# Attention with a top-32 mask and a feed-forward network in one kernel: a slot's transposes, the values of the slot ahead and later scores are put behind one another on TensorE

## The chip, the cores and the metric

The kernel runs on one core of one Trainium2 chip. The metric is the time of one execution in microseconds (us) as the device measures it. The core's engines are TensorE (PE in the rows; PEld are its weight loads), VectorE (DVE), ScalarE (ACT), GpSimd (POOL) and the queue that issues transfers (SP). Each works through its own instructions in order and waits on semaphores for the others.

## The reference

```python
# q, k, v: batch 8, heads 8, sequence 576, head_dim 64, float32
scores = scale * np.matmul(q, k.transpose(0, 1, 3, 2))
kth = np.partition(scores, -32, axis=-1)[..., -32:-31]
scores = np.where(scores >= kth, scores, -1e9)
scores = scores - np.max(scores, axis=-1, keepdims=True)
attn = np.exp(scores)
attn = attn / (np.sum(attn, axis=-1, keepdims=True) + 1e-09)
x = np.matmul(attn, v)                 # heads side by side: 4608 tokens x 512
a, b = x @ w1, x @ w2                  # 512 x 1024 each
out = (a * b @ w3) @ w_out             # 1024 x 1024, 1024 x 512
```

## The kernel before, in words

The work is cut into **slots**. A slot is 128 query rows of one pair of heads of one batch entry (or, at the ends of the sequence, 64 rows of two pairs). There are 18 slots per batch entry and 144 in all. Twelve slots fill a **block**: 384 columns of x, for which the feed-forward network is then computed with 288 matmuls of 384 columns. The weights w3 and w_out are folded into one matrix at the start, and weights, x and g are split into a high and a low part, so that three matmuls stand for one product.

One round p of the main loop (line 514) works on four slots at once, each at another stage. The scores of slot p+1 are made by `scores` (TensorE, into two tiles st) and copied to s by `take_scores` (ScalarE), in two halves. The 32 largest values of slot p are found by `top32_steps` (VectorE), whose parts the loop calls with `next(finder)`. For slot j = p-1, `edges_of` (GpSimd) prepares threshold and maximum, `mask` (ScalarE, then GpSimd) masks, and `exps` (ScalarE) takes the exponentials and their sums, head by head. For slot m = p-2, `invert` (VectorE) and `normalise` (ScalarE) divide, `turn` transposes the weights on TensorE (eight transposes into tp, a ninth, the tail, into ro), `take_turned` (ScalarE) copies both out as pts and pr, and `values` (TensorE) multiplies them with v. The result ov is split into x by `split_high` (ScalarE) and `split_low` (VectorE).

Between these stages `fill(8)` stands three times a round. It first calls `evict`, which issues the copies and products that wait for finished feed-forward groups (asb, g, osb: ScalarE, VectorE, GpSimd), and then 8 matmuls of the block whose turn it is. `begin` takes a finished block into that queue. `warm` does the same for the loading and decoding of weights, in the first rounds alone; in those no feed-forward runs. Every instruction keeps the order of the program on its engine (class `InOrder`), so what stands in the loop is what each engine does, in that order.

The tiles tp and st share a pool of two buffers in PSUM (`ps_a`); ro and ov share one. The array of TensorE is used whole (128x128) by the transposes and the feed-forward, as two halves of 64 rows (64x128) by the scores, and as two halves of 64 columns (128x64) by the values.

Of the kernel before, what the change touches and what calls it, by code (L numbers as in the profile page):

```python
# [9 lines left out]
F32 = mybir.dt.float32  # L10
# [8 lines left out]
B, H, S, D = 8, 8, 576, 64  # L19
# [49 lines left out]
def attn_moe(ctx: ExitStack, tc: tile.TileContext, q, k, v, w1, w2, w3, w_out, out, flag, any_missed, general):  # L69
# [39 lines left out]
    def stir(n):  # L109
        idle = ps_e.tile([128, 512], F32, tag="pf", name="idle", bufs=1)  # L110
        for _ in range(n):
            pe.matmul(idle[:, :128], ident, ident, start=True, stop=True)
# [69 lines left out]
    def at(x, b, *i):  # L182
        return x[(b, *i)] if isinstance(b, int) else x[(ds(b, 1), *i)].rearrange("o p n -> (o p) n")

    def load_q(b, t, split=False):
        qt = att_p.tile([128, NHP * 128], F32, tag="q", name="qt")
        for cut in (slice(0, 128), slice(128, NHP * 128)) if split else (slice(0, NHP * 128),):
            sp.dma_start(qt[:, cut], at(q, b, t)[:, cut])
        return qt

    def load_k(b, hp):
# [69 lines left out]
        return edge  # L261

    def new_weights():
        return att_p.tile([128, 2, S], F32, tag="pab", name="pab"), small.tile([128, 2], F32, tag="sums", name="sums")

    def mask(s, edge, pab, a, after=None):
        act.activation(pab[:, a, :], s[:, a, :], AF.Relu, bias=edge[:, a, 1:2], scale=-STEEP)
# [18 lines left out]
        for a in range(2):  # L286
            act.activation(pab[:, a, :], pab[:, a, :], AF.Copy, scale=rec[:, a : a + 1])

    def turn(pab):
        tp = ps_a.tile([128, 2, 512], F32, tag="a", name="tp")  # L290
        flat = pab[:].rearrange("p a c -> p (a c)")
        for a in range(2):
            for c in range(4):
                o = a * (S + 64) + c * 128
                pe.transpose(tp[:, a, c * 128 : (c + 1) * 128], flat[:, o : o + 128], ident)
        ro = ps_v.tile([128, 512], F32, tag="v", name="ro")
        pe.transpose(ro[:, :128], flat[:, 512:640], ident)
        return tp, ro

    def take_turned(tp, ro):  # L300
        pts = att_p.tile([128, 2, 512], F32, tag="pts", name="pts", bufs=1)
        act.copy(pts, tp)
        pr = att_p.tile([128, 128], F32, tag="pr", name="pr", bufs=1)
        act.copy(pr, ro[:, :128])
        return pts, pr

    def values(vts, hps, pts, pr, ro):
        ov = ro[:, 256:384]
        ends = len(hps) == 2
        for j, hp in enumerate(hps):  # L310
            vt = vts[hp]
            for c in range(5):
                for i, h in enumerate(HEADS):
                    block = i * 4 + c if c < 4 else (((8, 10), (10, 9))[j][i] if ends else 8 + i)
                    n = HEADS[i ^ j] if ends else slice(0, 128)
                    rhs = pr[:, n] if c == 4 else pts[:, j if ends else i, c * 128 + n.start : c * 128 + n.stop]
                    to = ov[h, j * 64 : j * 64 + 64] if ends else ov[h]
                    pe.matmul(to, vt[:, block * D : (block + 1) * D], rhs, start=(c == 0), stop=(c == 4))
        return ov
# [14 lines left out]
    def split_low(high, low, whole):  # L334
        dve.tensor_tensor(low, whole, high.bitcast(F32), op=ALU.subtract)
# [49 lines left out]
    if general:  # L385
        outs = out.rearrange("e (b t) -> b e t", b=B)
        for src, step in startup:
            for _ in step(fetch(src)):
                pass
        settle()  # L390
        with tc.For_i(0, B, 1) as b:
            seen = small.tile([1, 1], I32, tag="seen", name="seen", bufs=1)
            nc.sync.dma_start(seen, flag[ds(b + 1, 1), :])
            with tc.If(nc.values_load(seen, min_val=0, max_val=1) > 0):
                kts = {hp: load_k(b, hp) for hp in range(NHP)}
                vts = {hp: load_v(b, hp) for hp in range(NHP)}
                for first, ts in ((0, range(3)), (NB, range(3, TAIL + 1))):
                    xs, lo = [new_x(0) for _ in range(NHP)], 0
                    for t in ts:
                        qt = load_q(b, t)  # L400
                        for hps in [hps for hps, u in slots_of(0) if u == t]:
                            s, st = new_s(), scores(qt, kts, hps)
                            for h in range(2):
                                take_scores(s, st, h)
                            edge = top32_exact(s)
                            pab, sums = new_weights()
                            for a in range(2):
                                mask(s, edge, pab, a)
                                exps(edge, pab, sums, a)
                            add_up(sums)  # L410
                            invert(sums)
                            normalise(pab, sums)
                            tp, ro = turn(pab)
                            pts, pr = take_turned(tp, ro)
                            ov = values(vts, hps, pts, pr, ro)
                            for part in parts_of([xs[hp] for hp in hps], lo, t, ov):
                                split_high(*part)
                                split_low(*part)
                        lo += width(t)
                    place = lambda es: outs[ds(b, 1)][:, es, first : first + lo].rearrange("o p n -> (o p) n")  # L420
                    for _ in moe_steps(xs, lo, [(place, slice(0, lo))], lambda f: f()):
                        pass
        return
# [57 lines left out]

    def renew_q(g):
        if g < len(groups):
            qts[g] = load_q(*groups[g], g == 0)

    waiting = list(startup)
    fetched, going = [], []
# [16 lines left out]
        prefetch(WAITING)  # L504

    renew_q(0)
    stir(8)
    kts[0, 0] = load_k(0, 0)
    prefetch(4)
    kts[0, 1] = load_k(0, 1)  # L510
    kts[0, 2] = load_k(0, 2)
    kts[0, 3] = load_k(0, 3)
    renew_q(1)
    for p in range(-1, n_slots + 3):
        i, j, m = p + 1, p - 1, p - 2
        if p == 1:
            vts[0, 0] = load_v(0, 0)
            vts[0, 1] = load_v(0, 1)
            vts[0, 2] = load_v(0, 2)
            vts[0, 3] = load_v(0, 3)  # L520
        finder = top32_steps(ss[p], p) if 0 <= p < n_slots else iter(())
        if 0 <= m < n_slots:
            invert(pabs[m][1])
        folded = next(finder, None)
        for part in fresh:
            split_low(*part)
        fresh.clear()
        warm()
        if 0 <= j < n_slots:
            edges[j] = edges_of(j)  # L530
        if 0 <= m < n_slots:
            normalise(*pabs[m])
        if 0 <= j < n_slots:
            pabs[j] = new_weights()
            for a in range(2):
                mask(ss[j], edges[j], pabs[j][0], a, folded if a == 0 else None)
        warm()
        fill(SHARE[0])
        begin()
        next(finder, None)  # L540
        if 0 <= m < n_slots:
            tp, ro = turn(pabs[m][0])
            pts, pr = take_turned(tp, ro)
        if 0 <= j < n_slots:
            exps(edges[j], *pabs[j], 0)
        warm()
        fill(SHARE[1])
        next(finder, None)
        warm()
        if i < n_slots:  # L550
            b, hps, t = slots[i]
            st = scores(qts[group_of[i]], of(kts, b), hps)
            ss[i] = new_s()
            take_scores(ss[i], st, 0)
        if 0 <= j < n_slots:
            exps(edges[j], *pabs[j], 1)
        if i < n_slots:
            take_scores(ss[i], st, 1)
            renew(kts, load_k, i)
            if i + 1 == n_slots or group_of[i + 1] != group_of[i]:  # L560
                renew_q(group_of[i] + 2)
        if 0 <= m < n_slots:
            b, hps, t = slots[m]
            ov = values(of(vts, b), hps, pts, pr, ro)
            renew(vts, load_v, m)
        if p == 13:
            stir(9)
        next(finder, None)
        warm()
        fill(SHARE[2])  # L570
        for _ in finder:
            pass
        if 0 <= m < n_slots:
            n = m // BLOCK
            for hp in hps:
                if (n, hp) not in xs:
                    xs[n, hp] = new_x(n)
            fresh += parts_of([xs[n, hp] for hp in hps], column[group_of[m]], t, ov)
            for part in fresh:
                split_high(*part)  # L580
            del ss[m], pabs[m], edges[m]
            if (m + 1) % BLOCK == 0:
                starting.append(n)
        if p == 2:
            stir(8)
        if 0 <= j < n_slots:
            add_up(pabs[j][1])
        warm()
    begin()
# [67 lines left out]
```

## Time and profile before

| | |
|---|---|
| median of 3 runs | 1254.57 us (1254.1 to 1254.63) |
| the profiled execution's own time | 1254.34 us |
| its span, first to last instruction | 1252.4 us |
| TensorE busy | 1211.6 us (97%) |
| VectorE busy | 1147.6 us (92%) |
| ScalarE busy | 1107.9 us (88%) |
| GpSimd busy | 693.0 us (55%) |

The span counts from the first instruction to the last; the time of an execution holds a little more around it. A busy engine is one with an instruction under way; since instructions overlap, busy time says little of the room that is left, and the starts of successive instructions say more. The first 165 us belong to the decoding of weights, the last 50 us to the feed-forward of the last block alone; between them lie 130 slots of equal make.

### The profile page before, as it was taken

The page shows a single profiled execution, that of the slowest core. Times are in us where ns is not written, and L with a number is a line of the kernel's source. Part 1 is how long each engine was busy: PE and PEld are TensorE (multiplying, and loading weights), DVE is VectorE, ACT ScalarE, POOL GpSimd, SP SyncE. Part 2 cuts the span into 40 slices and gives each one's busy share as a digit, 9 for nine tenths or more (in the row PEclk, how much of TensorE's full clock was granted, in tenths as well). Part 3 has the DMA queues.
Part 4 walks back from the last instruction along what each step waited for, and adds up shares of the span by engine and source line. Part 5 has one row for each costly group of instructions (what it writes and reads, how often), then busy time and mean ns, then how long its engine had stood idle before and what let it go on. Part 6 is the DMA issues. An engine that isn't in the chain of part 4 may idle for free.

```text
span 1252.4 us, 27210 instructions
## 1 busy us (share of the span) xinstructions
PE 1211.6 (97%) x9419; PEld 1032.4 (82%) x9419; DVE 1147.6 (92%) x3952; ACT 1107.9 (88%) x2233; POOL 693.0 (55%) x877
## 2 busy tenths in 40 slices
PE   3899799999999999999999999999999999999998
PEld 2554378888888888888888888888888888888998
DVE  7999999999999999999999999999999999999710
ACT  5899999999999999999999999999999999999921
POOL 3688766556556556556556556556556556556510
PEclk7899899999999999999999999999999999999999
DMA  7344302000210012000210012000210012000000
GB/s 289 110 144 152 109 32 84 21 24 21 75 46 10 22 45 84 22 23 21 76 46 10 23 45 83 22 23 21 76 46 10 23 46 84 22 23 1 14 13 27
DMA packets 30258, 64.71 MB, mean 52 GB/s; under 512 B 5412, under 2 KB 11812, under 8 KB 30116
## 3 DMA queue, kind: packets, MB, share of 16 engines
q1 hardware_dynamic: 30116, 62.93, 15.4%
q8 instruction: 75, 1.23, 0.4%
q14 instruction: 67, 0.55, 0.1%
HBM read 53.48 MB, written 9.44 MB: 50 GB/s over the span
## 4 chain that ended last, share of the span: by engine, by line
PE 88%; DVE 5%; ACT 4%; POOL 2%; issue 1%; POOLq 0%; ACTq 0%
PE ab L58 34%; PE eo L58 17%; PE ro L58 15%; PE st L58 12%; PE tp L58 9%; ACT pab L58 2%; DVE w L58 2%; POOL z L58 1%; DVE top L58 1%; ACT z L58 1%; DVE z L58 1%; ACT pts L58 1%; POOL wl L58 1%; DVE t L58 1%; PE pf L58 1%
## 5 line engine op out<-in xcount | busy, mean ns | idle before, releaser
L58 POOL TENSOR_TENSOR pab<-s,pab 128x576 f32<-128x576 f32 x288 | 404.9, 1427 | 247.5 <-ACT pab L58 229.3
L58 DVE MAX8 top<-w 128x8 f32<-128x192 f32 (+1 forms) x1152 | 467.3, 447 | 0.0
L58 PE MATMUL ab<-x,wh 128*128 128x384 f32 x1536 | 402.9, 343 | 0.3 <-DVE wl L58 0.3
L58 DVE MATCH_REPLACE8 w<-top,w 128x192 f32<-128x192 f32 x864 | 289.7, 343 | 0.0
L58 PEld LDWEIGHTS ab<-x,wh 128*128 128x128 f32 x1536 | 273.9, 188 | 0.5 <-DVE wl L58 0.5
L58 PE MATMUL ab<-x,wl 128*128 128x384 f32 x768 | 268.4, 350 | 0.0
L58 ACT ACTIVATE pab<-pab,edge 128x576 f32<-128x576 f32 x288 | 227.1, 789 | 1.8 <-POOL pab L58 1.8
L58 PE MATMUL eo<-g,wf 128*128 128x384 f32 x1152 | 225.6, 345 | 0.0
L58 ACT ACTIVATE pab<-pab,sums 128x576 f32<-128x576 f32 x288 | 211.3, 795 | 8.2 <-DVE sums L58 8.1
L58 ACT COPY pts<-tp 128x1024 f32<-128x1024 f32 x144 | 145.9, 1013 | 74.1 <-PE tp L58 73.9
L58 ACT ACTIVATE pab<-s,edge 128x576 f32<-128x576 f32 x288 | 208.7, 784 | 1.9 <-POOL edge L58 1.9
L58 PEld LDWEIGHTS eo<-g,wf 128*128 128x128 f32 x1152 | 198.5, 188 | 7.5 <-issue 7.5
L58 PE MATMUL st<-kt,qt 64*128 64x288 f32 (+1 forms) x1280 | 186.0, 436 | 10.2 <-ACT pts L58 5.4
L58 ACT COPY s<-st 128x576 f32<-128x576 f32 x288 | 185.0, 643 | 8.7 <-PE st L58 8.7
L58 PEld LDWEIGHTS ro<-pts,vt 128*64 128x64 f32 x2560 | 128.9, 138 | 57.0 <-ACT g L58 34.7
L58 PE MATMUL tp<-ident,pab 128*128 128x128 f32 x1152 | 152.3, 276 | 18.7 <-ACT pab L58 18.7
L58 DVE TENSOR_TENSOR w<-s 128x384 f32<-128x384 f32 x288 | 150.4, 562 | 15.8 <-ACT s L58 7.7
L58 DVE TENSOR_TENSOR w<-w,s 128x384 f32<-128x384 f32 x288 | 159.4, 553 | 4.9
L58 PE MATMUL ro<-pts,vt 128*64 128x128 f32 (+1 forms) x2560 | 163.0, 271 | 0.0
L58 POOL TENSOR_TENSOR g<-asb,g 128x384 fp32r<-128x384 f32 x96 | 96.7, 1008 | 119.6 <-ACT g L58 119.6
L58 PEld LDWEIGHTS tp<-ident,pab 128*128 128x128 f32 x1152 | 135.9, 142 | 31.6 <-ACT pab L58 24.7
L58 PEld LDWEIGHTS ab<-x,wl 128*128 128x128 f32 x768 | 143.9, 187 | 13.4 <-issue 12.3
(50 smaller groups left out, 1133.1 us busy)
## 6 DMA issues: line engine op xcount, KB each, us to landing
z<-in_w SPq DMA_DIRECT2D x32, 512.0 KB, 3.6
vt<-in_v SPq DMA_DIRECT2D x32, 352.0 KB, 3.4
kt<-in_k SPq DMA_DIRECT2D x32, 320.0 KB, 3.2
qt<-in_q SPq DMA_DIRECT2D x39, 256.0 KB, 2.7
out_t<-osb SPq DMA_DIRECT2D x32, 192.0 KB, 1.9
z<-in_wo SPq DMA_DIRECT2D x8, 512.0 KB, 6.6
out_t<-osb SPq DMA_DIRECT2D x16, 160.0 KB, 1.8
out_t<-osb SPq DMA_DIRECT2D x16, 32.0 KB, 1.6
```

The lines of the kernel that those rows point to most:

```text
L58: ins = fn(*args, **kw)
```

## The change

From the slot after the first block to the last but one (`together(m)`), the order within a round is another.

- The tail is transposed ahead of the other eight (`turn(pab, ahead)`), into the tile vo, and pr is copied at once, by `take_tail`. The second head's mask goes behind it on ScalarE.
- `values` of the slot ahead (m-1, so p-3) stand right behind the transposes, and the scores of slot p+1 right behind these. All 24 feed-forward matmuls of a round follow one another.
- ro and ov were a tile that is taken anew in each slot; they are now two places in one lasting tile, vo.
- The exponentials of the second head stand ahead of `split_high` and the evictions of the second `fill`; the second half of the score copies is the last that ScalarE does in a round. `split_low` goes to the end of VectorE's search.
- pts is written over the slot's own weights pab, which therefore have three buffers, pr two. q has one buffer, is loaded in one transfer and a group later than before. At the start 6 instead of 8 matmuls of the identity are issued.

The flags `True` and `False` in the loop are constants.

```diff
-    def load_q(b, t, split=False):
-        qt = att_p.tile([128, NHP * 128], F32, tag="q", name="qt")
-        for cut in (slice(0, 128), slice(128, NHP * 128)) if split else (slice(0, NHP * 128),):
-            sp.dma_start(qt[:, cut], at(q, b, t)[:, cut])
+    def load_q(b, t):
+        qt = att_p.tile([128, NHP * 128], F32, tag="q", name="qt", bufs=1)
+        sp.dma_start(qt, at(q, b, t))
         return qt
...
-        return att_p.tile([128, 2, S], F32, tag="pab", name="pab"), ...
+        return att_p.tile([128, 2, S], F32, tag="pab", name="pab", bufs=3), ...
...
-    def turn(pab):
+    vo = ps_v.tile([128, 512], F32, name="vo")
+
+    def turn(pab, ahead):
         tp = ps_a.tile([128, 2, 512], F32, tag="a", name="tp")
         flat = pab[:].rearrange("p a c -> p (a c)")
+        ro = vo[:, :128]
+        if ahead:
+            pe.transpose(ro, flat[:, 512:640], ident)
         for a in range(2):
             for c in range(4):
                 o = a * (S + 64) + c * 128
                 pe.transpose(tp[:, a, c * 128 : (c + 1) * 128], flat[:, o : o + 128], ident)
-        ro = ps_v.tile([128, 512], F32, tag="v", name="ro")
-        pe.transpose(ro[:, :128], flat[:, 512:640], ident)
+        if not ahead:
+            pe.transpose(ro, flat[:, 512:640], ident)
         return tp, ro
 
-    def take_turned(tp, ro):
-        pts = att_p.tile([128, 2, 512], F32, tag="pts", name="pts", bufs=1)
+    def take_tail(ro):
+        pr = att_p.tile([128, 128], F32, tag="pr", name="pr")
+        act.copy(pr, ro)
+        return pr
+
+    def take_turned(pab, tp):
+        pts = pab[:].rearrange("p a c -> p (a c)")[:, :1024].rearrange("p (a c) -> p a c", a=2)
         act.copy(pts, tp)
...
-    stir(8)
+    stir(6)
...
+    def together(m):
+        return BLOCK <= m < n_slots - 1
+
+    def look(i):
+        if i < n_slots:
+            b, hps, t = slots[i]
+            seen[i] = scores(qts[group_of[i]], of(kts, b), hps)
+            ss[i] = new_s()
+            renew(kts, load_k, i)
+            if i + 1 == n_slots or group_of[i + 1] != group_of[i]:
+                renew_q(group_of[i] + 1)
+
+    def weigh(m):
+        b, hps, t = slots[m]
+        ovs[m] = values(of(vts, b), hps, *turned.pop(m))
+        renew(vts, load_v, m)
...
     for p in range(-1, n_slots + 3):
...
         if 0 <= j < n_slots:
             pabs[j] = new_weights()
-            for a in range(2):
-                mask(ss[j], edges[j], pabs[j][0], a, folded if a == 0 else None)
+            mask(ss[j], edges[j], pabs[j][0], 0, folded)
+            if not together(m):
+                mask(ss[j], edges[j], pabs[j][0], 1)
         warm()
         fill(SHARE[0])
         begin()
+        if 0 <= m < n_slots:
+            tp, ro = turn(pabs[m][0], together(m - 1))
+            if together(m - 1):
+                pr = take_tail(ro)
+        if 0 <= j < n_slots and together(m):
+            mask(ss[j], edges[j], pabs[j][0], 1)
         next(finder, None)
         if 0 <= m < n_slots:
-            tp, ro = turn(pabs[m][0])
-            pts, pr = take_turned(tp, ro)
+            pts = take_turned(pabs[m][0], tp)
+            turned[m] = pts, pr if together(m - 1) else take_tail(ro)
+            if together(m) and not together(m - 1):
+                fill(SHARE[0])
+        if together(p - 3):
+            weigh(p - 3)
+        if together(m):
+            look(i)
         if 0 <= j < n_slots:
             exps(edges[j], *pabs[j], 0)
+        if together(m):
+            take(i, 0)
+        if together(m) and True:
+            if 0 <= j < n_slots:
+                exps(edges[j], *pabs[j], 1)
+                add_up(pabs[j][1])
+        if together(p - 3):
+            spread(p - 3)
+        if together(m) and False:
+            take(i, 1)
         warm()
         fill(SHARE[1])
         next(finder, None)
         warm()
...
-        if 0 <= m < n_slots:
-            b, hps, t = slots[m]
-            ov = values(of(vts, b), hps, pts, pr, ro)
-            renew(vts, load_v, m)
+        if not (together(m) and False):
+            take(i, 1)
+        if 0 <= m < n_slots and not together(m):
+            settle_low()
+            weigh(m)
...
+        if together(p - 3):
+            settle_low()
+        if 0 <= m < n_slots and not together(m):
+            spread(m)
```

`spread` holds what stood at the end of the round before: it takes the tiles of x, calls `split_high` and, at a block's last slot, puts the block on the list from which `begin` takes it. `settle_low` holds the calls of `split_low`.

In three places the order of the instructions is shown. First TensorE in a regular slot before, from the end of one run of feed-forward (ab) through transposes (tp, ro), scores (st) and values (ro) to the next:

```order
L58 MATMUL ab<-x,wl_1221 128x384
L58 MATMUL tp<-ident,pab 128x128 x8
L58 MATMUL ro<-ident,pab 128x128
L58 MATMUL ab<-x,wh_102 128x384 x2
L58 MATMUL ab<-x,wl_107 128x384
L58 MATMUL ab<-x,wh_102 128x384 x2
L58 MATMUL ab<-x,wl_107 128x384
L58 MATMUL ab<-x,wh_102 128x384 x2
L58 MATMUL st<-kt,qt 128x288 x4
L58 MATMUL ro<-pts,vt 64x128 x8
L58 MATMUL ro<-pr,vt 64x128 x2
L58 MATMUL ab<-x,wl_107 128x384
```

Eight feed-forward matmuls stand between transposes and scores, and the values are those of the slot just transposed; each matmul of the scores and the values shows as two in the trace. Now TensorE where the first block of the changed kernel ends, from the last feed-forward matmuls of it (eo) to the first of the next block (ab); a regular slot reads the same but for its feed-forward:

```order
L58 MATMUL eo<-g,wf_105 128x384
L58 MATMUL eo<-g,wf_104 128x384
L58 MATMUL vo<-ident,pab 128x128
L58 MATMUL tp<-ident,pab 128x128 x8
L58 MATMUL vo<-pab,vt 64x128 x8
L58 MATMUL vo<-pr,vt 64x128 x2
L58 MATMUL st<-kt,qt 128x288 x4
L58 MATMUL vo<-ident,pab 128x128
L58 MATMUL tp<-ident,pab 128x128 x8
L58 MATMUL vo<-pab,vt 64x128 x8
L58 MATMUL vo<-pr,vt 64x128 x2
L58 MATMUL st<-kt,qt 128x288 x4
```

Transposes, values and scores stand behind one another, and two slots of them follow each other with no feed-forward between; in the kernel before, 24 such matmuls lie in every round from the first block on. Counted over the whole order, 16 stand ahead of these two slots where 24 stood, 32 in the first round of the block where 24 stood, and behind the small transpose near the end 272 where 248 stood. Last ScalarE in a round of the changed kernel, from normalising to normalising (pr is the tail's copy, pab<-tp that of the other transposes, pab,sums the exponentials):

```order
L58 ACTIVATE pab<-pab,sums 128x576 x2
L58 ACTIVATE pab<-s,edge 128x576
L58 COPY pr<-vo 128x128
L58 ACTIVATE pab<-s,edge 128x576
L58 COPY pab<-tp 128x1024
L58 ACTIVATE pab,sums<-pab,edge 128x576
L58 COPY s<-st 128x2x288
L58 ACTIVATE pab,sums<-pab,edge 128x576
L58 CAST x<-vo 128x128
L58 COPY osb<-eo 128x384
L58 COPY s<-st 128x2x288
L58 ACTIVATE pab<-pab,sums 128x576 x2
```

Before, the two masks stood together, pr behind pts, and the cast of g or copy of osb and the first score copy between the two exponentials.

## Rows read from the trace of the kernel before

**Rows 1.** Busy time by stretch: PE, PEld, DVE, ACT, POOL, granted clock, DMA.

```profile
400.00:600.00 200.00, 200.00 (x1667) 176.51 (x1666) 194.03 (x687) 185.59 (x378) 110.57 (x145) 1.00 0.11 36
```

**Rows 2.** Who waited for whom, 400 to 1150 us: total, times, longest.

```profile
PEld ro L58 <- ACT g L58: 25.3, 64, 0.4
PEld st L58 <- issue: 23.6, 96, 0.3
DVE sums L58 <- POOL sums L58: 13.9, 32, 0.4
...
PEld ab L58 <- issue: 8.7, 51, 0.2
```

**Rows 3.** Timeline of TensorE, one slot: start, duration, instruction, count.

```profile
524.56 3.09 PE L58 MATMUL eo<-g,wf 128*128 128x384 f32 x16
527.49 1.03 PE L58 MATMUL tp<-ident,pab 128*128 128x128 f32 x8
528.36 0.27 PE L58 MATMUL ro<-ident,pab 128*128 128x128 f32 x1
528.38 1.65 PE L58 MATMUL eo<-g,wf 128*128 128x384 f32 x8
529.97 1.24 PE L58 MATMUL st<-kt,qt 64*128 64x288 f32 x8
531.14 1.09 PE L58 MATMUL ro<-pts,vt 128*64 128x128 f32 x16
...
532.38 0.44 PE L58 MATMUL eo<-g,wf 128*128 128x384 f32 x1
```

**Rows 4.** Timeline of VectorE about the end of a slot with a and b.

```profile
571.64 0.17 DVE L58 RECIPROCAL sums<-sums 128x2 f32<-128x2 f32 x1
571.87 0.56 DVE L58 TENSOR_TENSOR w<-s 128x384 f32<-128x384 f32 x1
```

**Rows 5.** Timeline of ScalarE, the slot that ends there.

```profile
564.05 1.48 ACT L58 ACTIVATE pab<-pab,sums 128x576 f32<-128x576 f32 x2
565.40 1.46 ACT L58 ACTIVATE pab<-s,edge 128x576 f32<-128x576 f32 x2
566.73 0.49 ACT L58 COPY asb<-ab 128x384 f32<-128x384 f32 x1
567.66 1.01 ACT L58 COPY pts<-tp 128x1024 f32<-128x1024 f32 x1 [0.43 <-PE tp L58]
568.57 0.27 ACT L58 COPY pr<-ro 128x128 f32<-128x128 f32 x1
...
571.87 0.81 ACT L58 ACTIVATE pab<-pab,sums 128x576 f32<-128x576 f32 x1
```

**Rows 6.** Timeline of TensorE in the first rounds: the last transpose and the scores.

```profile
88.80 0.27 PE L58 MATMUL ro<-ident,pab 128*128 128x128 f32 x1
89.00 0.76 PE L58 MATMUL st<-kt,qt 64*128 64x288 f32 x4
```

**Rows 7.** Timeline of TensorE: feed-forward matmuls behind the last slot.

```profile
1196.81 0.52 PE L58 MATMUL ab<-x,wh 128*128 128x384 f32 x2
1197.16 0.34 PE L58 MATMUL ab<-x,wl 128*128 128x384 f32 x1
1197.34 0.51 PE L58 MATMUL ab<-x,wh 128*128 128x384 f32 x2
```

**Rows 8.** TensorE by stretch in the first rounds: length, busy, granted clock, DMA.

```profile
139.00:142.50 3.50, 1.12 (x2) 0.99 0.47 150
142.50:146.00 3.50, 2.56 (x11) 0.50 0.82 275
```

**Rows 9.** Timeline of the start: TensorE and VectorE.

```profile
1.73 3.78 PE L58 MATMUL idle<-ident 128*128 128x128 f32 x16 [1.73 <-POOL ident masks.py:199]
5.45 1.46 PE L58 MATMUL st<-kt,qt 64*128 64x288 f32 x8
7.68 1.03 DVE L58 TENSOR_TENSOR w<-s 128x384 f32<-128x384 f32 x2 [7.68 <-ACT s L58]
```

More of the change, by code (lines that the diff above doesn't have):

```diff
@@ L263, in new_weights @@
     def new_weights():
-        return att_p.tile([128, 2, S], F32, tag="pab", name="pab"), small.tile([128, 2], F32, tag="sums", name="sums")
+        return att_p.tile([128, 2, S], F32, tag="pab", name="pab", bufs=3), small.tile([128, 2], F32, tag="sums", name="sums")
     def mask(s, edge, pab, a, after=None):
@@ L295, in turn, with values @@
                 pe.transpose(tp[:, a, c * 128 : (c + 1) * 128], flat[:, o : o + 128], ident)
-        ro = ps_v.tile([128, 512], F32, tag="v", name="ro")
-        pe.transpose(ro[:, :128], flat[:, 512:640], ident)
+        if not ahead:
+            pe.transpose(ro, flat[:, 512:640], ident)
         return tp, ro
-    def take_turned(tp, ro):
-        pts = att_p.tile([128, 2, 512], F32, tag="pts", name="pts", bufs=1)
-        act.copy(pts, tp)
[L303 to L308, printed above, removed]
+    def take_tail(ro):
[4 more added lines that the diff above has]
+        pts = pab[:].rearrange("p a c -> p (a c)")[:, :1024].rearrange("p (a c) -> p a c", a=2)
+        act.copy(pts, tp)
+        return pts
+    def values(vts, hps, pts, pr):
+        ov = vo[:, 256:384]
         ends = len(hps) == 2
@@ L412, in attn_moe @@
                             normalise(pab, sums)
-                            tp, ro = turn(pab)
-                            pts, pr = take_turned(tp, ro)
-                            ov = values(vts, hps, pts, pr, ro)
+                            tp, ro = turn(pab, False)
+                            pts, pr = take_turned(pab, tp), take_tail(ro)
+                            ov = values(vts, hps, pts, pr)
                             for part in parts_of([xs[hp] for hp in hps], lo, t, ov):
@@ L483, in renew_q @@
         if g < len(groups):
-            qts[g] = load_q(*groups[g], g == 0)
+            qts[g] = load_q(*groups[g])
     waiting = list(startup)
@@ L512, in attn_moe, with take, spread, settle_low @@
     kts[0, 3] = load_k(0, 3)
-    renew_q(1)
+    turned, seen, ovs = {}, {}, {}
+    def together(m):
[8 more added lines that the diff above has]
+                renew_q(group_of[i] + 1)
+    def take(i, h):
+        if i < n_slots:
+            take_scores(ss[i], seen[i], h)
+    def weigh(m):
+        b, hps, t = slots[m]
+        ovs[m] = values(of(vts, b), hps, *turned.pop(m))
+        renew(vts, load_v, m)
+    def spread(m):
+        b, hps, t = slots[m]
+        n = m // BLOCK
+        for hp in hps:
+            if (n, hp) not in xs:
+                xs[n, hp] = new_x(n)
+        fresh[:] = parts_of([xs[n, hp] for hp in hps], column[group_of[m]], t, ovs.pop(m))
+        for part in fresh:
+            split_high(*part)
+        del ss[m], pabs[m], edges[m]
+        if (m + 1) % BLOCK == 0:
+            starting.append(n)
+    def settle_low():
+        for part in fresh:
+            split_low(*part)
+        fresh.clear()
     for p in range(-1, n_slots + 3):
@@ L524, in attn_moe @@
         folded = next(finder, None)
-        for part in fresh:
-            split_low(*part)
-        fresh.clear()
+        settle_low()
         warm()
@@ L539, in attn_moe @@
         begin()
+        if 0 <= m < n_slots:
[4 more added lines that the diff above has]
+            mask(ss[j], edges[j], pabs[j][0], 1)
         next(finder, None)
         if 0 <= m < n_slots:
-            tp, ro = turn(pabs[m][0])
-            pts, pr = take_turned(tp, ro)
+            pts = take_turned(pabs[m][0], tp)
[6 more added lines that the diff above has]
+            look(i)
         if 0 <= j < n_slots:
             exps(edges[j], *pabs[j], 0)
+        if together(m):
[8 more added lines that the diff above has]
+            take(i, 1)
         warm()
@@ L549, in attn_moe @@
         warm()
[L550 to L555, printed above, removed]
-            exps(edges[j], *pabs[j], 1)
[L557 to L561, printed above, removed]
-        if 0 <= m < n_slots:
-            b, hps, t = slots[m]
-            ov = values(of(vts, b), hps, pts, pr, ro)
-            renew(vts, load_v, m)
+        if not together(m):
+            look(i)
+            take(i, 0)
+        if 0 <= j < n_slots and not (together(m) and True):
+            exps(edges[j], *pabs[j], 1)
+        if not (together(m) and False):
[3 more added lines that the diff above has]
+            weigh(m)
         if p == 13:
@@ L572, in attn_moe @@
             pass
[L573 to L583, printed above, removed]
+        if together(p - 3):
+            settle_low()
+        if 0 <= m < n_slots and not together(m):
+            spread(m)
         if p == 2:
             stir(8)
-        if 0 <= j < n_slots:
+        if 0 <= j < n_slots and not (together(m) and True):
             add_up(pabs[j][1])
```

## The prediction

> **What bounds the kernel now.** I read the engines' busy time in a stretch of the steady part first [rows 1]: TensorE is busy for 200.00 of 200 us, VectorE for 194.03, ScalarE for 185.59. Three engines are nearly full, so I looked next at who waits for whom between 400 and 1150 us [rows 2]. The reader is to see that TensorE's matmuls wait for no other engine there: what stands in the list for it are weight loads, held once before the scores (23.6 us over 96 slots, 0.25 each), once before the values (25.3 over 64, 0.39) and once before the feed-forward matmuls that follow the values (8.7 over 51, 0.17). ACT g stands as releaser of the second only because it ended last; it gives the values nothing. VectorE waits 0.43 us a slot, but only in 32 of 96 slots (13.9 us).
>
> The timeline of TensorE in one slot [rows 3] gives the slot's sum. F stands for feed-forward matmuls (ab and eo), T for the nine transposes, S for the scores, V for the values. From start to start: 16 F 2.93, T 0.89, 8 F 1.59, S 1.17, V 1.24: 7.82 us, and the slots follow one another without a gap. So TensorE sets the pace. VectorE in a slot with its product of a and b [rows 4] ends its reciprocal at 571.81 and starts the next search at 571.87: 0.06 us to spare, 7.76 of work; without the product 7.82 - 0.43 = 7.39. ScalarE's slot [rows 5] runs from 564.05 to 571.87 with one wait of 0.43: 7.39 of work. A slot's time can thus hardly fall below 7.76 in the two thirds of the slots that compute a and b (192 of a block's 288 F), nor below 7.4 in the others, whatever TensorE saves.
>
> **The change part by part.** *The regular slot.* It was T, 8 F, S, V, 16 F; it becomes T, V (of the slot ahead), S, 24 F, in 131 slots. No matmul goes and none comes. What can change is the breaks where the shape of TensorE's array tile changes: T and F use 128x128, S 64x128, V 128x64. Before there were three: F to S, S to V, V to F; between T and F, both 128x128, there is none. After there are again three: T to V, V to S, S to F. Their price goes by rows. T has a pitch of (528.36 - 527.49) / 8 = 0.109 us [rows 3]. In the start T stood right ahead of S: there the first scores start 0.20 after the last transpose [rows 6], 0.09 over the pitch. So T costs 8 x 0.109 + 0.20 = 1.07. V and S each with the break behind it stay 1.24 and 1.17 if a break depends on what ends, and F has a pitch of 0.53 / 3 = 0.177 [rows 7]: 24 F are 2.93 + 8 x 0.177 = 4.35. Sum: 1.07 + 1.24 + 1.17 + 4.35 = 7.83, or +0.01 a slot, +1.3 us over 131 slots.
>
> T to V and V to S are not in the trace of before. At the least they cost nothing: -0.09 and -0.17, -0.26 a slot. At the most each costs what the dearest break does, 0.39: +0.30 and +0.22, +0.5 a slot. I take the +0.01, whose nearest row is T to S.
>
> A rule speaks to this. The Trainium skill (TensorEngine Tiling (Array Packing), Key Properties) says that changing the tiling mode, and not just the tile, drains TensorE. By that rule both new neighbours drain as the old ones did, and the sum stays at 7.83; without it it could be 7.57. The rows on S, V and F agree with it (0.25, 0.39, 0.17); no row shows the two new pairs.
>
> *The waits.* V now stands behind T, and it writes the same tile vo that the pr copy of this slot reads, so it waits for that copy. Therefore the tail is transposed first. It is done 0.27 after T begins; the copy takes 0.27 [rows 5], so V, due at 1.07, is not late. Behind pr on ScalarE stand one mask (0.67, half of the two from 565.40 to 566.73) and pts, which waits for all of T: it ends at about 1.2 + 1.01 = 2.2 after T's begin. The second half of S needs it, for its buffer, at 1.07 + 1.24 + 0.6 = 2.9. It has 0.7 to spare. The score copies need S, which ends at 3.5; before the second of them ScalarE now has pts, two exponentials and the x and g casts, so it is there later than that and does not wait. ScalarE has 7.83 - 7.39 = 0.44 a slot for its new waits, and pr and pts take most of it. If pr comes late, V has 1.07 - 0.6 = 0.5 more before TensorE stops. Queued behind V would be S and all F; behind pr all of ScalarE, and VectorE's next search behind the last score copy. VectorE's low part of x goes from the middle of the search to its end: same work. On GpSimd the g difference now stands ahead of the next edges; the mask that needs these stands on ScalarE behind 1.35 us of normalising (564.05 to 565.40), which covers it. On SP the loads of v that follow V now go out ahead of those of k and q in a round, and the stores of out later than both; each is needed a slot later at the earliest, so I cost them at nothing.
>
> *The blocks start a slot later.* A slot's values are now finished one round later, so block 1 begins its F in round 27 and not 26. In round 14 eight F are pulled ahead and V is put off: 8 x 0.177 - 1.24 = +0.2 us. The first block then runs dry: the order shows T V S T V S with no F between. 32 F, 5.7 us of TensorE's work, are missing there, but the two slots can't be shorter than VectorE's 7.39 each: 2 x (7.82 - 7.39) = -0.9 us. The balance of 24 F stands at the very end, behind the last slot, where nothing lies beside it: 24 x 0.177 = +4.25 us. The order shows 272 F behind the last small transpose, 248 before.
>
> *The clock.* In that hole TensorE idles 5.7 - 0.9 = 4.8 us, most of it at a stretch. Between 139 and 142.5 us it was busy for 1.12 of 3.5 us, and the granted clock was 0.50 right behind, 1.2 of 2.4 GHz [rows 8]. If that recurs, the next T, V and S (3.48) take up to twice as long: 0 to +3.5. I take the middle, +1.7.
>
> *Start.* 12 idle matmuls instead of 16, at (5.45 - 1.73) / 16 = 0.23, and q in one transfer: the first scores can come up to 0.9 earlier, or not at all if they wait for the transfers instead. VectorE, whose first work waits for them until 7.68 [rows 9], gains 0 to 0.9; I take -0.4. With one buffer for q its load goes out when the last scores of a group are read; they are next needed a slot later, some 7 us. In-place pts frees space only.
>
> Sum: 1.3 + 0.2 - 0.9 + 4.25 + 1.7 - 0.4 = +6.2. On the profiled execution's 1254.34 (its span is 1252.4 and 1.9 lies around it; the median of the runs is 1254.57, 0.2 above) that is 1260.5; I say 1260.
>
> **The rivals.**
> *The new pairs don't break (faster).* For it: they are not in the trace, and weight loads are busy only 176.51 of 200 us [rows 1]. Against it: every change of shape that is there costs. At -0.26 a slot: 44 slots gain 0.26, 87 slots 0.06, since VectorE then sets the pace: -11 - 5 = -16 instead of +1.3. That gives 1243; with half of the saving, 1251. The Trainium skill (Perfetto Trace Analysis, Identifying the Most-Contended Engine) holds matmul busy time a bad measure of TensorE's room and weight-load time a good one; by it 12% would be open here. The rows show where those 12% lie, in the breaks, which the change moves and doesn't remove.
>
> *ScalarE and VectorE take over (slower still).* They hang in one ring: reciprocal, normalising, ScalarE's slot up to the last score copy, the next search. The place is the pr copy: it has to wait for T, and each us that ScalarE stands there before and can't make up comes later at VectorE, which has 0.06. It decides when ScalarE's new waits pass 0.44 a slot in the slots with a and b; every 0.1 beyond gives 87 x 0.1 = 9 us. At 0.1 to 0.2 beyond: 1269 to 1278. For it: the small reserves. Against: V bears another 0.5, and the slots with eo make up.
>
> *The late block costs little (no change).* If the two slots shrink by more than I allow and the clock holds, and the start gives its 0.9: 1254.3 + 1.3 + 0.2 - 2 + 4.25 - 0.9 = 1257; with a little gained at the breaks, 1255.
>
> **How the numbers follow.** The forecast has 0.5 (own range 1257 to 1264), the missing breaks 0.26, the ring 0.12, no change 0.12. A measurement of this kernel can tell about 0.2%, 2.5 us, from no change: 1252.1 to 1257.1. Faster: 0.26 less the smallest of the savings, 0.25. Within: 0.12 and the edges of both neighbours, 0.17. Slower: 0.58. The range reaches from 1242 to 1269: it leaves out savings beyond 0.26 a slot, the ring from 0.1 on and the dearest breaks (+0.5 a slot, +65 us, against which T to S speaks), about 0.2.
>
> **What would show it.** Right: TensorE's slots of 7.8 with T, V, S, F in that order and about 1.07, 1.24, 1.17, 4.35; a hole of some 4 us in the slots about 260 us from the start; feed-forward alone for about 52 us at the end instead of 48. Wrong: a slot below 7.7 in the slots with eo, with V close behind T; or TensorE waiting for the pr copy, pts or normalising in most slots.

## The result, and the profile after

The changed kernel takes 1262.19 us (median of 4 runs, 1261.93 to 1262.94), the kernel before 1254.46 on the same chip: ratio 1.0062, 95% interval 1.005 to 1.0075. It is slower by 7.7 us; the forecast was 1260.0, the range 1242 to 1269. The profiled execution has a span of 1260.57 us, 8.1 more than before (1252.44).

In the steady part the four engines are as full as before [rows 1] (the same columns, of the kernel after):

```profile
400.00:600.00 200.00, 200.00 (x1668) 178.12 (x1669) 195.00 (x684) 189.41 (x379) 113.91 (x146) 1.00 0.11 36
```

TensorE is again busy all the time. One slot on its timeline (after; start, duration, instruction, count), beside [rows 3]:

```profile
523.77 4.51 PE L58 MATMUL eo<-g,wf 128*128 128x384 f32 x24
528.11 0.27 PE L58 MATMUL vo<-ident,pab 128*128 128x128 f32 x1
528.22 1.03 PE L58 MATMUL tp<-ident,pab 128*128 128x128 f32 x8
529.19 1.09 PE L58 MATMUL vo<-pab,vt 128*64 128x128 f32 x16
530.11 0.39 PE L58 MATMUL vo<-pr,vt 128*64 128x128 f32 x4
530.43 1.24 PE L58 MATMUL st<-kt,qt 64*128 64x288 f32 x8
531.60 2.74 PE L58 MATMUL eo<-g,wf 128*128 128x384 f32 x14
```

The reader is to see the starts: T 528.11 to 529.19, 1.08; V to 530.43, 1.24; S to 531.60, 1.17; 24 F from 523.77 to 528.11, 4.34. Together 7.83 instead of 7.82. Which waits stand for TensorE from 400 to 1150 us (after: who waits for whom, total, times, longest), beside [rows 2]:

```profile
PEld ab L58 <- issue: 24.9, 63, 0.4
...
PEld vo L58 <- issue: 15.4, 92, 0.2
PEld st L58 <- PE vo L58: 14.4, 84, 0.2
...
PEld eo L58 <- issue: 12.3, 32, 0.4
```

Only weight loads are held, once at each change of the array's shape: 0.17 before V, 0.17 before S, and 0.39 before the F behind S (37.2 over 95). With the rows left out that is 0.71 a slot of 7.83; before it was 0.79 a slot of 7.82. The longest hold was before V and is now before F; there are three as there were. The time for which a load is held is not its price: 0.08 less of it a slot did not make the slot shorter.

So most of the 8.1 us lies outside the regular slot, as the starts of the transposes show, read from TensorE's timeline of both kernels (slots counted from 0):

| up to | before | after | added in the stretch | forecast |
|---|---|---|---|---|
| slot 0 | 28.94 | 27.96 | -0.98 | -0.4 |
| slot 10 | 143.27 | 143.34 | +1.05 | 0 |
| slot 13 (round 14 lies here) | 175.26 | 175.47 | +0.14 | +0.2 |
| slot 23 | 253.62 | 253.99 | +0.16 | +0.1 |
| slot 26 (the hole) | 277.08 | 277.33 | -0.12 | +0.8 |
| slot 141 | 1176.88 | 1178.55 | +1.42 | +1.2 |
| slot 143, the last | 1190.17 | 1192.73 | +0.89 | 0 |
| end of the span | 1252.44 | 1260.57 | +5.56 | +4.25 |

The first loss. In the first rounds TensorE waits for pts before the second half of the scores. TensorE before, then TensorE after, the same slot (in brackets the idle time and its releaser):

```profile
99.25 1.04 PE L58 MATMUL tp<-ident,pab 128*128 128x128 f32 x8
...
101.41 0.76 PE L58 MATMUL st<-kt,qt 64*128 64x288 f32 x4 [0.33 <-ACT pts L58]
```

```profile
98.78 1.04 PE L58 MATMUL tp<-ident,pab 128*128 128x128 f32 x8
99.66 0.27 PE L58 MATMUL vo<-ident,pab 128*128 128x128 f32 x1
...
101.09 0.76 PE L58 MATMUL st<-kt,qt 64*128 64x288 f32 x4 [0.47 <-ACT pab L58]
```

The wait grew from 0.33 to 0.47, and the slots from 11.34 to 11.47. ScalarE's copy in the same slot, before, then after (pts is now written over pab):

```profile
100.36 1.00 ACT L58 COPY pts<-tp 128x1024 f32<-128x1024 f32 x1
```

```profile
100.02 1.01 ACT L58 COPY pab<-tp 128x1024 f32<-128x1024 f32 x1
```

It starts 1.24 behind the beginning of T; before it was 1.11 (100.36 against 99.25). The difference is one transpose, the ninth.

The hole (after, by stretch, columns as above), and what the next transposes waited for:

```profile
263.50:268.00 4.50, 0.83 (x8) 0.33 (x4) 4.46 (x15) 4.08 (x10) 2.66 (x4) 0.96 0.19 58
268.00:271.80 3.80, 3.76 (x29) 3.28 (x29) 3.80 (x19) 3.02 (x5) 2.82 (x3) 0.60 0.00 0
```

```profile
268.04 0.47 PE L58 MATMUL vo<-ident,pab 128*128 128x128 f32 x1 [3.71 <-ACT pab L58]
```

Two slots shrank (6.67 and 7.38), and the third took 9.29, with T and V at a granted clock of 0.60 on the mean: for the most part at the lower of its two levels, 1.2 of 2.4 GHz.

The end (after, TensorE from the last but one transposes on):

```profile
1186.01 0.33 PE L58 MATMUL vo<-ident,pab 128*128 128x128 f32 x1 [0.65 <-ACT pab L58]
...
1192.73 0.27 PE L58 MATMUL vo<-ident,pab 128*128 128x128 f32 x1
1192.84 1.03 PE L58 MATMUL tp<-ident,pab 128*128 128x128 f32 x8
1193.80 1.09 PE L58 MATMUL vo<-pab,vt 128*64 128x128 f32 x16
1194.72 0.39 PE L58 MATMUL vo<-pr,vt 128*64 128x128 f32 x4
1195.04 1.67 PE L58 MATMUL eo<-g,wf 128*128 128x384 f32 x8
1196.64 1.09 PE L58 MATMUL vo<-pab,vt 128*64 128x128 f32 x16
1197.57 0.39 PE L58 MATMUL vo<-pr,vt 128*64 128x128 f32 x4
1197.89 7.33 PE L58 MATMUL eo<-g,wf 128*128 128x384 f32 x40
```

The values stand here twice: those of the last slot but one, which are a slot late, and those of the last. That is 1.24 more in front of the 24 F more; together they make 5.5 of the 5.56.

### The profile page after: what moved, and what is told of

It reads as the page before. It is cut to its first block, busy times and chain, and to the rows that moved or that the text cites. A ratio compares the mean times of both kernels' runs of the same rounds, so it can differ in the third digit from the quotient of the medians.

```text
span 1260.6 us, 27617 instructions
## 1 busy us (share of the span) xinstructions
PE 1214.0 (96%) x9415; PEld 1043.9 (83%) x9415; DVE 1153.3 (91%) x3952; ACT 1129.6 (90%) x2233; POOL 706.0 (56%) x877
## 4 chain that ended last, share of the span: by engine, by line
PE 82%; DVE 9%; ACT 6%; POOL 2%; issue 1%; POOLq 0%; ACTq 0%; DVEq 0%
PE ab L58 31%; PE eo L58 16%; PE vo L58 14%; PE st L58 11%; PE tp L58 9%; DVE w L58 4%; ACT pab L58 4%; DVE top L58 3%; POOL z L58 1%; ACT z L58 1%; POOL wl L58 1%; DVE z L58 1%; PE pf L58 1%; DVE t L58 1%; ACT wf L58 0%
## 5 line engine op out<-in xcount | busy, mean ns | idle before, releaser
L58 PE MATMUL ab<-x,wl 128*128 128x384 f32 x768 | 261.3, 340 | 0.0
L58 ACT ACTIVATE pab<-s,edge 128x576 f32<-128x576 f32 x288 | 221.3, 773 | 0.7 <-POOL edge L58 0.7
L58 PE MATMUL eo<-g,wf 128*128 128x384 f32 x1152 | 215.6, 343 | 0.0
L58 DVE TENSOR_TENSOR w<-s 128x384 f32<-128x384 f32 x288 | 170.1, 631 | 27.9 <-ACT s L58 26.6
L58 PE MATMUL vo<-pab,vt 128*64 128x128 f32 (+1 forms) x2560 | 163.4, 271 | 0.0
L58 PEld LDWEIGHTS tp<-ident,pab 128*128 128x128 f32 x1152 | 133.2, 143 | 31.1 <-ACT pab L58 22.9
L58 PEld LDWEIGHTS vo<-pab,vt 128*64 128x64 f32 x2560 | 129.3, 139 | 28.4 <-issue 23.4
L58 ACT COPY pab<-tp 128x1024 f32<-128x1024 f32 x144 | 145.0, 1007 | 4.2 <-PE vo L58 2.6
L58 PEld LDWEIGHTS st<-kt,qt 64*128 64x128 f32 (+1 forms) x1280 | 97.8, 179 | 58.4 <-PE vo L58 19.2
```

The lines of the kernel that those rows point to most:

```text
L58: ins = fn(*args, **kw)
```

## The experiments

All times are medians on chips that ran the kernel before beside them (1254.3 to 1254.7). Slots and stretches are read from one profiled execution of each.

**e1_apart: a fourth break.** Eight F go between V and S, and both copies of the scores behind the exponentials (the moved copies are not shown).

```diff
         if together(p - 3):
             weigh(p - 3)
+        if together(p - 3):
+            feed(SHARE[1])
         if together(m):
             look(i)
...
-        fill(SHARE[1])
+        fill(0 if together(p - 3) else SHARE[1])
```

> The changed kernel with eight of a round's feed-forward matmuls moved between the values and the scores, so that TensorE's array changes its shape four times a slot and not three; ScalarE takes both score copies behind the exponentials, so that it does not wait for the later scores. If the changes of shape cost about 0.2 us each whatever stands beside them (my theory), values to feed-forward (0.20) and feed-forward to scores (0.19) take the place of values to scores (0.20): 8.02 us a slot and not 7.83, +0.19 x 129 = +25, about 1287. If the ring of ScalarE and VectorE sets the slot, or the place of the matmuls makes no difference, slots stay at 7.83 to 7.9 and the time at 1262 to 1270.

1290.44 us, ratio to before 1.0292 (1.0276 to 1.0307). One slot on TensorE (e1_apart):

```profile
645.05 0.27 PE L58 MATMUL vo<-ident,pab 128*128 128x128 f32 x1
645.16 1.03 PE L58 MATMUL tp<-ident,pab 128*128 128x128 f32 x8
646.13 1.09 PE L58 MATMUL vo<-pab,vt 128*64 128x128 f32 x16
647.05 0.39 PE L58 MATMUL vo<-pr,vt 128*64 128x128 f32 x4
647.37 1.67 PE L58 MATMUL eo<-g,wf 128*128 128x384 f32 x8
648.97 1.24 PE L58 MATMUL st<-kt,qt 64*128 64x288 f32 x8
650.14 3.09 PE L58 MATMUL eo<-g,wf 128*128 128x384 f32 x16
653.07 0.27 PE L58 MATMUL vo<-ident,pab 128*128 128x128 f32 x1
```

The slot is 8.02: T 1.08, V 1.24, 8 F 1.60, S 1.17, 16 F 2.93. Each piece is as long as in the other orders, and one break more costs 0.185 (21.2 us between slots 26 and 141, 115 slots), though weight loads are held 0.25 longer a slot. That bears out the sum of the regular slot. Another 5.4 us came before slot 21, in seven slots of 8.6 each. There the rival "ScalarE and VectorE take over" can be seen (e1_apart, waits from 184 to 243 us):

```profile
ACT g L58 <- DVE asb L58: 4.3, 7, 0.6
PE vo L58 <- ACT pr L58: 3.5, 7, 0.5
```

ScalarE stands for VectorE's product of a and b, so the pr copy is late, and V waits for it in all seven. In the regular slots of the changed kernel TensorE waits for pr nowhere.

**e2_no_hole: blocks start a round earlier.** `begin` is called right behind `spread`, and the low halves are made there.

```diff
             spread(p - 3)
+            if starting:
+                settle_low()
+                begin()
...
-            if together(m) and not together(m - 1):
-                fill(SHARE[0])
```

> The changed kernel, but a finished block enters the feed-forward queue in the round that splits its last slot, ahead of that round's second eight matmuls, and the eight pulled ahead in round 14 go back. Joined transposes, values and scores stay. If the late blocks carry most of the loss (my theory): 24 matmuls of 0.177 less at the end, -4.25; round 14 gets its 24 matmuls instead of 32 and loses its values to a later round, -0.9; the hole near 262 us goes with its half clock, +0.1: about 1257, slots still 7.83. If the loss lies in the joining itself, the time stays within 1.5 us of 1262.

1292.22, ratio 1.0315 (1.0297 to 1.0333): a miss of mine. The low half, put in the middle of VectorE's search, waits for ScalarE's high half (VectorE, e2_no_hole):

```profile
265.79 0.29 DVE L58 TENSOR_TENSOR x<-vo,x 128x128 fp32r<-128x128 f32 x1 [3.64 <-ACT x L58]
```

Each of 10 block starts took a slot of 10.33 instead of 7.83: of the wait inside the search, 2.5 of 3.64 came through. Behind five of them the next slot took 9.4 to 9.6, in all five at a granted clock of about 0.7 on the mean of 5 us. The end behind the last transposes is 63.6 us here, 4.2 less than in the changed kernel.

**e2b_no_hole: the same without that wait.** In that round the search is finished first.

```diff
             spread(p - 3)
+            if starting:
+                begin()
+                new = True
...
+        if new:
+            for _ in finder:
+                pass
+            settle_low()
         fill(SHARE[2])
```

> Block work begins in the round in which its last values are spread, and round 14 has no eight F more; in that one round of each block the low halves are made behind the whole of VectorE's search, so no wait stands inside the search (the fault of e2_no_hole). Theory (what the change loses is the 24 F that come to stand behind the last slot, and eight F in round 14): 1262.2 - 24 x 0.177 (4.25) - 0.85 in round 14 + 0.1 where the two short slots go = 1257.2, with the transposes of all regular slots 7.83 apart. What is left over the kernel before (+2.8) is then the values that come back at the end (1.24), the last-but-one round (0.8) and the first rounds. Rival (the end is set by the last slots' chain through ScalarE, VectorE and GpSimd, and fewer F behind it only leave TensorE idle there): 1261 to 1263.

1258.07, ratio 1.0031 (1.0019 to 1.0044): 4.1 less than the changed kernel. The hole is closed and the clock stays (e2b_no_hole, by stretch):

```profile
263.50:268.00 4.50, 4.50 (x36) 3.85 (x33) 3.94 (x15) 4.39 (x11) 1.61 (x4) 1.00 0.26 87
268.00:271.80 3.80, 3.80 (x39) 3.48 (x37) 3.77 (x14) 3.63 (x7) 2.20 (x2) 1.00 0.05 18
```

From the last transposes to the end 63.7 us instead of 67.8: the 24 F, 4.1. From slot 23 to slot 26 it takes 23.50 us against 23.34, so in the profiled execution of the changed kernel hole and half clock together had even given 0.16. Of the 0.9 over what I expected, 0.5 is a later start and 0.2 lies in round 14. The values still stand twice at the end (e2b_no_hole, TensorE):

```profile
1193.70 1.09 PE L58 MATMUL vo<-pab,vt 128*64 128x128 f32 x16
...
1196.54 1.09 PE L58 MATMUL vo<-pab,vt 128*64 128x128 f32 x16
```

**e3_tail_first: the tail first in all slots.**

```diff
-            tp, ro = turn(pabs[m][0], together(m - 1))
+            tp, ro = turn(pabs[m][0], True)
```

> The changed kernel with the tail transposed first in the first rounds too (it is so already in the others). There pts is written over the weights and has to wait for the ninth transpose, 0.13 us later than before, and rounds 3 to 10 take 11.47 instead of 11.34. If that wait sets the first rounds (my theory): 11.34 again, -1.05, about 1261.1. If they are slower for another reason (q's single buffer, another order on ScalarE): no change, 1262.2.

1263.52, ratio 1.0079 (1.0065 to 1.0093), 1.3 more than the changed kernel; slots 3 to 9 still 11.47 apart. The edit could not tell: whichever transpose is last, pts, written over what all nine read, comes behind it. It also adds a wait: the tail is written into vo, from which VectorE still makes a low half (TensorE, e3_tail_first):

```profile
146.03 0.45 PE L58 MATMUL vo<-ident,pab 128*128 128x128 f32 x1 [4.25 <-DVE x L58]
```

The slot before it took 12.36 instead of 10.15, and 0.6 us of lateness was still there four slots later. Its profiled execution lost 1.2 more behind the hole, where this kernel does the same as the changed one (slots of 6.67 and 7.38, then 3.70 idle): the next slot took 10.46 instead of 9.29, because the clock stayed low for longer (e3_tail_first, by stretch):

```profile
269.00:272.80 3.80, 3.72 (x25) 3.40 (x27) 3.80 (x19) 3.02 (x6) 2.86 (x3) 0.50 0.00 0
272.80:276.00 3.20, 3.20 (x20) 2.23 (x17) 1.55 (x3) 1.49 (x4) 0.00 (x0) 0.72 0.00 0
```

In the changed kernel the clock was 0.60 in the first of these stretches (from 268.0) and 1.00 in the second.

**e3b_own_pts: pts in a tile of its own in the first twelve slots.** To make room for it, the pool of asb and osb is opened later.

```diff
-            pts = take_turned(pabs[m][0], tp)
+            pts = take_turned(pabs[m][0], tp, m < BLOCK)
```

> In the first twelve slots the turned weights get a tile of their own, as in the kernel before, in place of being written over the weights that were turned. Theory (in the first rounds the copy of the turned weights, written in place, has to wait for the ninth transpose, and scores and values behind it start 0.13 us later in each of eight rounds): the transposes of rounds 3 to 10 come 11.34 apart as before, 1.05 less in all: 1261.1. Rival (the 0.13 comes from another part of the change, such as one bank for both small results): rounds 3 to 10 stay 11.47 apart, 1262.2.

1261.74, ratio 1.0066 (1.0052 to 1.008). TensorE and ScalarE (e3b_own_pts):

```profile
97.51 1.04 PE L58 MATMUL tp<-ident,pab 128*128 128x128 f32 x8
...
99.68 0.76 PE L58 MATMUL st<-kt,qt 64*128 64x288 f32 x4 [0.34 <-ACT pts L58]
```

```profile
98.63 0.99 ACT L58 COPY pts<-tp 128x1024 f32<-128x1024 f32 x1
```

pts starts 1.12 behind T, the wait is 0.34 again, and slots 3 to 9 come 11.32 behind one another: 1.15 gained from slot 2 to slot 10. In the median no more than 0.45 of it shows, within the run-to-run spread; the start alone (slot 0 at 27.9 to 28.9 us in the kernels that share it) moves by as much.

**e4b_both: the last two together** (both diffs above).

> The edits of e2b_no_hole and e3b_own_pts together. If both losses are separate stretches of one chain on TensorE they add up: 1257.2 - 1.05 = 1256.1, so still 1.6 over the kernel before (the values that come back at the end 1.24, the wait of the last-but-one round 0.8, less the earlier start). Rival (the start's gain is taken up again further on): as e2b_no_hole, 1257.2.

1256.85 (10 runs), ratio 1.0024 (1.0014 to 1.0033): 1.2 less than e2b_no_hole, so the two losses add up. What is left over before, 2.6 in the medians and 1.9 in the profiled spans, is made up in these spans as follows: from the last transposes to the end 63.74 us against 62.28 (the second V), 1.4 in 115 regular slots, 0.4 in the last two, less 1.4 that the start and round 14 gave.

**e5_warm: keep TensorE busy in the hole.**

```diff
+        if p == 26:
+            idle = late["mm"].tile([128, 512], F32, tag="mm", name="idle2")
+            for _ in range(16):
+                pe.matmul(idle[:, :128], ident, ident, start=True, stop=True)
```

> The changed kernel with 16 matmuls of the identity behind the scores of round 26, where TensorE otherwise has nothing for about 4 us. If the half clock of the next transposes and values costs what their longer times show (9 transposes 2.11 instead of 1.07, values 1.67 instead of 1.24; my theory): -1.4, about 1260.8, the granted clock stays 1.0 there. If the slot behind the hole is set by VectorE anyway, no change.

1260.9, ratio 1.0055 (1.0041 to 1.0069): 1.3 less. The stretch that stood at 0.60 (e5_warm):

```profile
268.00:271.80 3.80, 3.80 (x38) 2.98 (x37) 3.80 (x19) 3.79 (x8) 2.79 (x2) 1.00 0.00 0
```

The slot of 9.29 is 7.88. The half clock cost 1.4 us in the profiled execution of the changed kernel. It is not the same each time: in e3_tail_first that slot took 10.46.

**e6_exp_late: the second exponential behind the evictions**, a part of the change that moves work on ScalarE, and its sum on GpSimd, and none on TensorE.

```diff
-        if together(m) and True:
+        if together(m) and False:
```

> The second exponential pass goes back behind the evictions of the block work, the rest stays. Theory (TensorE waits for no other engine in a regular slot, so this part of the change moves nothing): 1262.2 +- 0.7, slots 7.83. Rival (the pass behind the evictions delays sums, their inverse and so the scaled weights that the next round's transposes read): a wait of 0.1 to 0.3 us in front of the transposes, times 130 slots: 1275 to 1301.

1262.08, ratio 1.0067 (1.0053 to 1.0081): no change, slots 7.83. VectorE now waits for the sums in 59 slots from 400 to 1150 us (18.8 in all), and TensorE for nothing.

**e7_before_start: the kernel before with the start of the changed one.**

```diff
-    stir(8)
+    stir(6)
...
-            qts[g] = load_q(*groups[g], g == 0)
+            qts[g] = load_q(*groups[g])
```

> The kernel before, with the start of the changed one alone: six matmuls on the identity in place of eight at the front, and the first queries in one transfer. Theory (what the change gained is its earlier first slot, 0.98 us, and it loses that again and more further on; in the first rounds of the kernel before nothing takes it up, as e4b_both showed by keeping 1.1 us up to the tenth slot): 1254.3 - 1.0 = 1253.3. Rival (the start varies from run to run by as much as that, 27.9 to 28.9 us in the runs of the changed kernel, and the edit itself moves nothing): 1254.3 +- 0.4.

1253.14 (11 runs) beside 1254.7, ratio 0.9987 (0.9978 to 0.9996): the one version whose interval lies below the kernel before, though by little. In its profile slot 0 begins at 27.92, and all slots to the last 1.0 to 1.15 earlier than before. Slot 2 comes at 52.2 to 53.4 us in all eleven kernels with this start, and at 53.95 before. VectorE's and TensorE's start (e7_before_start), beside [rows 9]:

```profile
4.59 1.30 PE L58 MATMUL st<-kt,qt 64*128 64x288 f32 x8
```

```profile
6.67 1.03 DVE L58 TENSOR_TENSOR w<-s 128x384 f32<-128x384 f32 x2 [6.67 <-ACT s L58]
```

**e9_start_warm: that, and nine idle matmuls more where TensorE idles in the first rounds.**

```diff
-        if p == 13:
+        if p in (11, 13):
             stir(9)
```

> As e7_before_start, and nine matmuls on the identity more behind the values of the slot that is turned at 133.3 us, so that TensorE does not idle from 137.4 to 140.0 and the granted clock may stay at 1.0 where it was 0.50 (142.5 to 153). Theory (VectorE is busy for 4.00 of every 4.00 us there and sets these rounds, so a faster TensorE gives nothing): as e7_before_start, within 0.4. Rival (TensorE's half-speed transposes, scores and values, 8.7 us of work at 0.5, set these rounds): up to 4.3 less, 1249.

1253.68, ratio 0.9994 (0.9985 to 1.0003). The clock behind the idle time rose from 0.50 [rows 8] to 0.89 (e9_start_warm):

```profile
142.50:146.00 3.50, 2.59 (x13) 1.27 (x13) 3.47 (x7) 3.20 (x6) 2.79 (x5) 0.89 0.81 290
```

The slots stay as they were (10.03, 12.69, 9.55 against 10.01, 12.69, 9.55). VectorE, busy for 3.47 of 3.50, sets these rounds; the 3.5 us in which the clock stayed up were worth nothing. From 146 to 149.5 us it was 0.50 here too, so a clock that stays up through all of these rounds was not tested.

## Why the prediction was right, and where it was not

**The regular slot: right, to the size.** I forecast 7.82 to 7.83, and TensorE's starts show that. Its ground, three breaks before and three after, is shown from both sides: the held weight loads of the profile after, and e1_apart, where a fourth break costs 0.185. The pairs T to V and V to S, which no row of before showed, hold the load for 0.17 each. That agrees with the Trainium skill (TensorEngine Tiling (Array Packing), Key Properties), which says that a change of the tiling mode drains TensorE. The rival "the new pairs don't break" falls with it. Weight loads are idle for 21.9 of 200 us after, 11%, and held loads make up 0.71 of each 7.83, 9 of those 11%; the change got nothing out of them. The Trainium skill (Perfetto Trace Analysis, Identifying the Most-Contended Engine), on which this rival drew, takes weight-load busy time as a measure of TensorE's room; for this change it was none.

**The waits: right for the regular slot.** TensorE waits for no copy in it. The rival "ScalarE and VectorE take over" did not come about, but it is near: e1_apart brought it on.

**The late block: right, the largest term.** 24 F at the end were sized at 4.25, and e2b_no_hole, which takes them away, ends 4.1 sooner behind the last transposes. The two slots of the hole gave 1.6 instead of 0.9, and the clock took 1.4 (e5_warm) where I said 1.7, the middle of 0 to 3.5. That these two are so close is in part luck: in e3_tail_first the clock took 1.2 more behind the same hole.

**Round 14: the term that was mis-sized.** I wrote 8 x 0.177 - 1.24 = +0.2 for it and measured +0.14, but V "put off" was booked as a saving and never paid back in the sum. A lag by one slot is paid at the end, where the last two V stand: +1.24, seen in the rows of after, e2b_no_hole and e4b_both.

**Missed: "in-place pts frees space only".** It also makes pts wait for the ninth transpose. In the regular slot the tail goes first and nobody is late; in the first slots it is last, and there ScalarE and VectorE have no room (before, from 133 to 139 us, both are busy for 6.00 of 6.00), so 0.13 a slot came to 1.05. e3b_own_pts shows it in the slots.

**Missed: the last two slots, +0.89.** They make no scores, so TensorE has only 6.66 of work and VectorE comes first. With the block a slot late, VectorE's search there still holds a product of a and b, which it did not before. VectorE before, then after:

```profile
1181.40 0.15 DVE L58 RECIPROCAL sums<-sums 128x2 f32<-128x2 f32 x1
```

```profile
1179.94 0.55 DVE L58 TENSOR_TENSOR asb<-ab,asb 128x384 f32<-128x384 f32 x1
...
1184.27 0.16 DVE L58 RECIPROCAL sums<-sums 128x2 f32<-128x2 f32 x1
```

The reciprocal ends 2.9 later (1184.43 against 1181.55), of which 1.7 is lateness from the slots ahead. The product is about half of the loss: in e4b_both, where it is gone from this search, 0.43 is left. This was not tested alone, and e2b_no_hole, which lacks it too, still loses 0.72; why these two differ stays open.

**The start: under-sized,** -0.98 instead of -0.4; e7_before_start shows that this part alone is a gain, of 1.0 to 1.15 in its profile and 1.6 in the median (0.5 to 2.8 by the interval).

In sum the forecast's +6.2 and the span's +8.1 differ by 1.24 and 0.07 (end), 1.05 (pts), 0.89 (last slots) and 0.3 (regular slots), less 0.9 (hole), 0.6 (start) and 0.06 (round 14). So the total is off by 2 only because 3.5 of losses that I missed or put too low stand against 1.6 that came out better: the mechanism of the slot and of the late block was right, the small distance of the total is partly luck.

## What to carry to other kernels

When matmuls of several shapes are put into another order, count the changes of array shape in a period, and price each by the starts in the trace and not by the time for which a load is held; here nothing came of an order that kept the count. A step that is put off by a period is paid back at the end of the program, together with all that waits for it, where nothing hides it. A buffer that is reused in place takes on the waits of every reader of the old content: look at the slots with the least room, not at the regular ones.

## What the runs showed of the hardware

- At a change of shape the next weight load is held for a time that goes by the pair: 0.17 for T to V, V to S and V to F, 0.25 for F to S, 0.39 for S to V and S to F. The price is another: 0.08 less of it a slot (0.79 before, 0.71 after) gave nothing, and 0.25 more (e1_apart) cost 0.185.
- Behind the hole, where TensorE had 0.83 us of work in 4.5, the granted clock was 0.60 on the mean of the next 3.8 us, which cost 1.4 us (e5_warm); behind the same hole in e3_tail_first it was 0.50 and then 0.72, and the slot took 1.2 longer still. In the first rounds, where VectorE sets the pace, 3.5 us at 0.50 cost nothing (e9_start_warm).
- The start is not steady: the first transposes of kernels with the same start came between 27.9 and 28.9 us, so that one profile cannot tell a gain of 1 us there.
